# Two kilobytes of one key load, taken as a load of 119 rows and a load of 9 rows

## The chip, the cores and the metric

The kernel runs on one NeuronCore of one Trainium2 chip. The metric is the device time of one execution in microseconds (us), as the median of several runs; lower is better. The core has five engines that run on their own (TensorE, in the profile PE, with its weight loads as PEld; VectorE, DVE; ScalarE, ACT; GpSimd, POOL; SyncE, SP) and 16 DMA engines that move data between HBM and the on-chip memory SBUF, which has 128 partitions.

## What is computed

One decode step (one new token for each of 4 sequences) goes through two layers. Both layers use the same weights and the same caches: layer norm, grouped-query attention over a cache of 4096 positions with 32 query heads and 8 key/value heads, a residual, layer norm, a SwiGLU feed-forward block, a residual.

```
def _A_ref(x, k_cache, v_cache, wq, wo):
    q = (x @ wq).reshape(B, Sq, Hq, Dh).transpose(0, 2, 1, 3)
    k = jnp.repeat(k_cache, rep, axis=1)
    v = jnp.repeat(v_cache, rep, axis=1)
    scores = jnp.einsum("bhqd,bhkd->bhqk", q, k) * (Dh ** -0.5)
    p = _softmax(scores, axis=-1)
    o = jnp.einsum("bhqk,bhkd->bhqd", p, v)
    return o.transpose(0, 2, 1, 3).reshape(B, Sq, Hq * Dh) @ wo

def _B_ref(x, w1, w3, w2):
    h = _silu(x @ w1) * (x @ w3)
    return h @ w2

for layer in range(2):
    x = x + _A_ref(_layernorm(x), A_k_cache, A_v_cache, A_wq, A_wo)
    x = x + _B_ref(_layernorm(x), B_w1, B_w3, B_w2)
```

Everything is float32: B = 4, D = 512, Hq = 32, Hkv = 8, Sk = 4096, Dh = 128, F = 1792.

## The kernel before

All weights and both caches lie in one HBM array of 128 rows (`rows`), in the order in which layer 0 uses them. Positions in it are counted in units (`KB` = 256 float32, so 1 KB of each row, 128 KB over all rows). On the chip one tile, `space`, of 218 such units per partition takes all that is loaded. The table `LOADS` (lines 52 to 66) sets by hand every transfer of the program in order: first unit in HBM, number of units, first unit in `space`. A second pass over the table's later half reads most of the data again for layer 1, which goes through the groups backwards, from group 7 to group 0.

`pump` (lines 120 to 144) walks the table: as long as the next entry's place in `space` is free, it issues that transfer on SP's DMA queue (line 140) and notes where each tile now lies. `done` frees a tile's units after its last use in a layer and calls `pump` again. So the order of the transfers is that of the table, and the moment of each is that at which the engine that last read the place has finished. The table's entry `(320, 64, 28)` is the transfer which the change touches: 64 units, 64 KB of each row, 8192 KB in all, to units 28 to 91 of `space`.

A group's keys are 64 units: 16 tiles of 4 units, 8 for each of two steps. So this entry holds all the keys of group 2, and its last two units (382 and 383) are the second half of the last tile of the second step. `score` (line 311) multiplies a step's key tiles with the queries, two matmuls for each tile, one for each half; `maximum`, `exponent` and `turn` make the softmax weights of it, and `weigh` (line 381) multiplies them with the group's values. Each layer ends with `feed_forward`, whose last part, `down` (line 499), reads the units of `w2` as they land (matmuls on line 503). Then DVE copies the result (line 599) and SP stores it (line 600).

Of the kernel before, what the change touches and what calls it, by code (L numbers as in the profile page):

```python
# [16 lines left out]
P = 128  # L17
# [25 lines left out]
KB = 256  # L43
# [16 lines left out]
    (868, 8, 68), (876, 4, 186), (880, 4, 190), (884, 8, 194), ("stash", 1, 202), (892, 8, 206), ("stash", 0, 214),  # L60
# [5 lines left out]
)  # L66
BUSY = (4, 1, 2)
SCRATCH = 64

# [5 lines left out]
def tile_decode_layers(ctx: ExitStack, tc: tile.TileContext, rows, out):  # L75
    nc = tc.nc
# [9 lines left out]
    def place(at, n):  # L86
        return space[:, at * KB:(at + n) * KB]
# [32 lines left out]
    def pump():  # L120
        while state["next"] < len(LOADS):
            src, n, at = LOADS[state["next"]]
            if src == "stash":
                i, n = n, U // KB
                keys = [("kv", TURN, i)]
                if i == 0 and not state["back"]:
                    return
            else:
                keys = [key for key in stream if src <= offset[key] < src + n]
            if any(taken[at:at + n]):  # L130
                return
            taken[at:at + n] = [True] * n
            if src == "stash":
                for j in range(2):
                    nc.scalar.activation(place(at, n)[:, j * BLOCK:(j + 1) * BLOCK], stored[2 * i + j], AF.Copy)
            elif state["next"] == 0:
                nc.sync.dma_start(space[:, at * KB:], rows[:, 0:n * KB + P])
            else:
                lo = src * KB + (P if src >= LOADS[0][1] else 0)
                nc.sync.dma_start(place(at, n), rows[:, lo:lo + n * KB])  # L140
            for key in keys:
                where[key] = at
                at += size[key[0]]
            state["next"] += 1
# [4 lines left out]
    def done(layer, *key):  # L149
        if layer == 0 and (key[0][:2] == "w1" or key[0] in ("wq", "wo") and key[1] >= HELD or key[:2] == ("kv", TURN) and key[2] in KEPT):  # L150
            return
        at, n = where[key], size[key[0]]
        taken[at:at + n] = [False] * n
        pump()

    pump()


# [40 lines left out]
    def busy(n):  # L199
        if n:  # L200
            pt = scores().rearrange("p (k c) -> p k c", k=KC)
            nc.tensor.matmul(pt[:, 0:n, :], ident, ident.unsqueeze(1).to_broadcast([P, n, P]),  # L202
                             start=True, stop=True)
# [31 lines left out]
    def layernorm():  # L235
        xc, sq = deviation()
        xT = lay_down(xc)
        squares(xc, sq)

        def factor():  # L240
            var = o_ps[1][:, 1:2]
            mean(var, ssq)
            inverse(rstd[:, 0:1], var)

        return xT, factor
# [173 lines left out]
    def turn_o(o, oT):  # L419
        nc.tensor.matmul(misc[:, 0:B * REP], o, head, start=True, stop=True)  # L420
        nc.vector.tensor_copy(oT[:, :, 0:B], misc[:, 0:B * REP].rearrange("p (b h) -> p h b", b=B))  # L421
# [5 lines left out]
    def project_o(layer, g, oT):  # L427
        w = wo_of(g)
        for h in range(REP):
            for k in range(KC):  # L430
                nc.tensor.matmul(x_ps[32 * k:32 * k + B, :], oT[:, h, 0:B], w[:, h, k * P:(k + 1) * P],  # L431
                                 start=(h == 0), stop=(h == REP - 1))
        done(layer, "wo", g)
        nc.vector.scalar_tensor_tensor(x_sb, x_ps, 1.0, x_sb, op0=ALU.mult, op1=ALU.add,
                                       accum_out=rowsum)
# [107 lines left out]
    for layer in range(LAYERS):  # L543
# [13 lines left out]
        for n, (g, (first, last)) in enumerate(order):  # L557
# [7 lines left out]
            if layer and n == 0:  # L565
                state["back"] = True
                pump()
# [22 lines left out]
        nc.scalar.activation(spare, half[:, 0:1], AF.Sigmoid)  # L590
        busy(BUSY[0])
        turn_o(o, oT)
        busy(BUSY[1])
        project_o(layer, g, oT)
        busy(BUSY[2])
        xT, factor = layernorm()
# [50 lines left out]
```

## Time and profile before

| what | value |
|---|---|
| median of 3 runs | 704.12 us (704.09 to 704.31) |
| the profiled execution, its own time | 704.12 us |
| its span, first to last instruction | 702.3 us |
| mean granted clock of TensorE | 0.825 |
| PE, PEld busy | 421.3 us, 133.4 us |
| DVE, ACT, POOL busy | 144.5 us, 41.7 us, 3.1 us |
| read from HBM | 297.34 MB |

The 1.8 us between the span and the execution's own time lie outside the profiled instructions. Times in the views below are microseconds from the start of the span. In a table of windows each row is a stretch of time: the busy time of each engine in it, the granted clock of PE, and the mean busy share of the 16 DMA engines with what they moved in GB/s. In a list of DMA queues a row has the packets, the MB and the time that the packets took as a share of 16 engines.

### The profile page before, as it was taken

Reading aid. Unit: us, or ns where it says so; the run is one execution under the profiler, and the core shown is the slowest. Engines: PE = TensorE matmul, PEld = TensorE weight load, DVE = VectorE, ACT = ScalarE, POOL = GpSimd, SP = SyncE. Lnnn points to the kernel's source line nnn. Section 1 sums busy time; section 2 is a strip of 40 time slices with the busy share of each in tenths; the row PEclk is TensorE's granted clock in tenths of the full one; section 3 lists DMA queues with packets and bytes.
Section 4 is the critical chain, followed back from the end, with each engine's and each line's share of the span. In section 5 each row is a group of like instructions: output and inputs, shape, how many; then the busy total and the mean of one; then the engine's idle time right before and its main releaser. Section 6 shows DMA issues by size and latency. Waiting matters only on the chain.

```text
span 702.3 us, 7502 instructions
## 1 busy us (share of the span) xinstructions
PE 421.3 (60%) x3280; PEld 133.4 (19%) x3280; DVE 144.5 (21%) x512; ACT 41.7 (6%) x100; POOL 3.1 (0%) x10
## 2 busy tenths in 40 slices
PE   1265466644578409667688985744555734567576
PEld 0111121201112103121124221201111211121223
DVE  2012112121023103330231322112120301213221
ACT  0010000100001001000101210000100001000100
POOL 0000000000000000000000000000000000000000
PEclk9997677876769859886999997877877958779999
DMA  9999999999999999999999999999999999999996
GB/s 422 418 415 425 467 419 418 426 457 417 449 414 444 424 438 415 436 423 427 422 418 378 423 430 440 439 438 418 441 440 414 450 419 448 430 425 417 424 425 268
DMA packets 12991, 297.87 MB, mean 424 GB/s; under 512 B 1440, under 2 KB 1568, under 8 KB 4512
## 3 DMA queue, kind: packets, MB, share of 16 engines
q1 hardware_dynamic: 12960, 297.41, 99.0%
q8 instruction: 25, 0.41, 0.2%
q14 instruction: 6, 0.05, 0.0%
HBM read 297.34 MB, written 0.07 MB: 423 GB/s over the span
## 4 chain that ended last, share of the span: by engine, by line
DMA 71%; PE 24%; DVE 1%; another core or an unknown queue 1%; ACT 1%; issue 1%; SPq 0%; ACTq 0%; DVEq 0%
DMA space<-in_rows 71%; PE o L387 10%; PE scores L322 9%; PE sums_ps L306 1%; PE turned L348 1%; ACT p L341 1%; PE scores L202 1%; PE stored L251 1%; DVE acc L335 0%; DVE pT L350 0%; PE o L463 0%; SPq L140 0%; PE sums_ps L431 0%; PE sums_ps L420 0%
## 5 line engine op out<-in xcount | busy, mean ns | idle before, releaser
L322 PE MATMUL scores<-space,qT 128*32 128x512 f32 x1024 | 170.0, 713 | 141.6 <-DMA space<-in_rows 140.8
L387 PE MATMUL o<-space,pT 128*16 128x512 f32 x1024 | 152.8, 710 | 99.3 <-DMA space<-in_rows 91.5
L322 PEld LDWEIGHTS scores<-space,qT 128*32 128x32 f32 x1024 | 36.0, 123 | 218.6 <-issue 180.0
L387 PEld LDWEIGHTS o<-space,pT 128*16 128x16 f32 x1024 | 31.7, 108 | 198.3 <-issue 94.2
L335 DVE TENSOR_REDUCE acc<-scores 128x1 f32<-128x512 f32 x32 | 22.1, 691 | 181.5 <-PE scores L322 181.5
L341 ACT ACTIVATE p<-scores,acc 128x512 f32<-128x512 f32 x30 | 20.6, 687 | 559.0 <-DVE acc L335 432.1
L410 DVE SCALAR_TENSOR_TENSOR o<-o,acc,o 128x128 f32<-128x128 f32 x112 | 39.3, 351 | 49.2 <-PE o L387 45.8
L350 DVE COPY pT<-turned 128x256 f32<-128x256 f32 x32 | 13.6, 425 | 154.3 <-PE turned L348 154.3
L348 PE MATMUL turned<-ident,p 128*128 128x128 f32 x128 | 21.9, 296 | 11.8 <-ACT p L341 11.8
L295 PE MATMUL sums_ps<-space,xT 128*32 128x512 f32 x120 | 22.9, 704 | 2.4 <-DMA space<-in_rows 2.4
L421 DVE COPY o<-sums_ps 128x16 f32<-128x16 f32 x16 | 2.8, 175 | 98.1 <-PE sums_ps L420 98.1
L348 PEld LDWEIGHTS turned<-ident,p 128*128 128x128 f32 x128 | 14.0, 145 | 44.1 <-ACT p L341 25.7
L306 PEld LDWEIGHTS sums_ps<-same,shares 128*128 128x128 f32 x120 | 16.3, 211 | 16.8 <-DVE shares L301 11.1
L306 PE MATMUL sums_ps<-same,shares 128*128 128x4 f32 x120 | 17.6, 270 | 0.9 <-DVE shares L301 0.9
L463 PE MATMUL o<-space,xT 128*32 128x192 f32 (+1 forms) x256 | 13.7, 355 | 3.2 <-DMA space<-in_rows 1.5
L441 PE MATMUL stored<-space,o 128*32 128x512 f32 x104 | 13.5, 592 | 0.0
L301 DVE TENSOR_SCALAR shares<-sums_ps,columns 128x512 f32<-128x512 f32 x15 | 11.1, 743 | 1.7 <-PE sums_ps L295 1.7
L503 PE MATMUL sums_ps<-space,hT 128*4 128x128 f32 x224 | 9.1, 272 | 3.6 <-DMA space<-in_rows 2.9
L211 PE MATMUL o<-columns,same 128*32 128x1 f32 x64 | 2.0, 181 | 14.3 <-DVE columns L548 13.3
L420 PEld LDWEIGHTS sums_ps<-columns,o 128*128 128x128 f32 x32 | 6.1, 239 | 20.6 <-issue 13.0
L463 PEld LDWEIGHTS o<-space,xT 128*32 128x32 f32 x256 | 7.6, 110 | 8.4 <-DVE h L480 2.8
L420 PE MATMUL sums_ps<-columns,o 128*128 128x16 f32 x32 | 7.7, 318 | 0.6 <-DVE o L410 0.6
(101 smaller groups left out, 141.9 us busy)
## 6 DMA issues: line engine op xcount, KB each, us to landing
space<-in_rows SPq DMA_DIRECT2D x11, 4096.0 KB, 21.6
space<-in_rows SPq DMA_DIRECT2D x14, 1024.0 KB, 18.6
space<-in_rows SPq DMA_DIRECT2D x3, 4608.0 KB, 24.6
space<-in_rows SPq DMA_DIRECT2D x2, 6144.0 KB, 30.9
space<-in_rows SPq DMA_DIRECT2D x6, 2048.0 KB, 29.2
space<-in_rows SPq DMA_DIRECT2D x3, 3584.0 KB, 23.5
space<-in_rows SPq DMA_DIRECT2D x2, 5120.0 KB, 28.7
space<-in_rows SPq DMA_DIRECT2D x1, 7680.0 KB, 33.8
```

Source lines behind the costliest of these rows:

```text
L295: nc.tensor.matmul(wide[32 * k:32 * k + 32, :], xT[:, 32 * k:32 * k + 32], w[:, k, :], start=True, stop=True)
L306: nc.tensor.matmul(misc[:, h * B:(h + 1) * B], shares[:, h * DH:(h + 1) * DH], same[:, 0:B], start=True, stop=True)
L322: nc.tensor.matmul(ps[32 * b:32 * b + 32, :], qT[:, b, at:at + 32], t[:, i * BLOCK:(i + 1) * BLOCK], start=(m < 2), stop=(m >= TILES - 2))
L335: nc.vector.tensor_reduce(acc[:, i:i + 1], ps, axis=AX.X, op=ALU.max, negate=True)
L341: nc.scalar.activation(p.rearrange("p n s -> p (n s)"), ps, AF.Exp, bias=acc[:, i:i + 1], scale=1.0 if scale is None else scale, accum_out ...
L348: nc.tensor.transpose(pt[:, n, :], p[:, n, :], ident)
L350: nc.vector.tensor_copy(pT, pt.rearrange("p n (b r) -> p n b r", b=B)[:, :, :, 0:ROW])
L387: nc.tensor.matmul(o_ps[i][32 * b:32 * b + ROW, :], pT[:, r // 2, b, :], t[:, j * NB * DH:(j + 1) * NB * DH], start=(r < 2), stop=(r >= TI ...
L410: nc.vector.scalar_tensor_tensor(o, o_ps[s][:, j * DH:(j + 1) * DH], acc[:, 16 + NB * s + j:17 + NB * s + j], o, op0=ALU.mult, op1=ALU.add)
L420: nc.tensor.matmul(misc[:, 0:B * REP], o, head, start=True, stop=True)
L441: nc.tensor.matmul(bank[32 * h:32 * h + 32, :], oT[:, h, :], w[:, h, :], start=first, stop=last)
L463: nc.tensor.matmul(bank[32 * j:32 * j + 32, s], xT[:, 32 * k:32 * k + 32], w[:, j], start=(k == 0), stop=(k == KC - 1))
```

## The change

The entry of 64 units becomes one of 62 units and one of 2 units, next to each other both in HBM and in `space`. A new table, `APART`, says for an entry how many of the 128 rows its first transfer takes; the remaining rows go in a second one. It has the one entry 382: 119.

```
@@ LOADS
-    (580, 28, 190), (320, 64, 28), (8, 24, 92), ...
+    (580, 28, 190), (320, 62, 28), (382, 2, 90), (8, 24, 92), ...
+APART = {382: 119}
@@ pump
                 lo = src * KB + (P if src >= LOADS[0][1] else 0)
-                nc.sync.dma_start(place(at, n), rows[:, lo:lo + n * KB])
+                cut = APART.get(src, P)
+                for rs in (slice(0, cut), slice(cut, P)):
+                    if rs.start < P:
+                        nc.sync.dma_start(place(at, n)[rs], rows[rs, lo:lo + n * KB])
```

All other entries have no row in `APART` and are issued as before, in one transfer of 128 rows. The same bytes go to the same places.

On SP's queue the entry stands among the loads of layer 1's groups 2 and 1. Each row is one transfer: rows of SBUF by float32 elements, and in brackets the semaphores that SP waits for ahead of it (`DMAHW` those of earlier transfers, `PE` those of matmuls). Before:

```order
L140 DMA space<-in_rows 128x9216 [waits DMAHW3_49,DMAHW1_49,PE_49]
L140 DMA space<-in_rows 128x7168 [waits PE_49]
L140 DMA space<-in_rows 128x16384 [waits DMAHW2_49,PE_49]
L140 DMA space<-in_rows 128x6144 [waits PE_49]
L140 DMA space<-in_rows 128x16384 [waits DMAHW4_49,DMAHW3_49,PE_49]
L140 DMA space<-in_rows 128x16384 [waits DMAHW5_49,DMAHW0_49,PE_49]
```

And with the change, where the transfer's line is 144:

```order
L144 DMA space<-in_rows 128x9216 [waits DMAHW3_49,DMAHW1_49,PE_49]
L144 DMA space<-in_rows 128x7168 [waits PE_49]
L144 DMA space<-in_rows 128x15872 [waits DMAHW2_49,PE_49]
L144 DMA space<-in_rows 119x512 [waits PE_49]
L144 DMA space<-in_rows 9x512
L144 DMA space<-in_rows 128x6144 [waits DMAHW0_49,PE_49]
L144 DMA space<-in_rows 128x16384 [waits DMAHW4_49,DMAHW3_49,PE_49]
```

The one transfer of 16384 elements has become three that follow each other, and every later one has moved back by two places; transfers take the eight `DMAHW` semaphores in turn, so the names behind it are shifted by two.

On PE the place is the end of group 2's second step in layer 1 and the start of its values. Before:

```order
L306 MATMUL sums_ps<-same,shares 128x4 [waits DVE_49]
L306 MATMUL sums_ps<-same,shares 128x4 x3
L322 MATMUL scores<-space,qT 32x512 x10
L387 MATMUL o_94<-space,pT 16x512 [waits DMAHW7_49]
L387 MATMUL o_94<-space,pT 16x512 x15
```

And with the change, with four lines more ahead of each:

```order
L310 MATMUL sums_ps<-same,shares 128x4 [waits DVE_49]
L310 MATMUL sums_ps<-same,shares 128x4 x3
L326 MATMUL scores<-space,qT 32x512 x9
L326 MATMUL scores<-space,qT 32x512 [waits DMAHW7_49,DMAHW6_49]
L391 MATMUL o_94<-space,pT 16x512 [waits DMAHW1_49]
L391 MATMUL o_94<-space,pT 16x512 x15
```

The step's last matmul, the only one that reads units 382 and 383, now waits for the two small transfers. The order of the matmuls is the same.

2 rows, old and new, of the table LOADS are left out of this document.

## The prediction

> **What bounds the kernel now.** I read the busy slices and the DMA queues first, then the chain of waits, then windows over the second half and over the last ten microseconds.
>
> ```profile
> DMA packets 12991, 297.87 MB, mean 424 GB/s; under 512 B 1440, under 2 KB 1568, under 8 KB 4512
> q1 hardware_dynamic: 12960, 297.41, 99.0%
> q8 instruction: 25, 0.41, 0.2%
> DMA 71%; PE 24%; DVE 1%; another core or an unknown queue 1%; ACT 1%; issue 1%; SPq 0%; ACTq 0%; DVEq 0%
> ```
>
> The loads' packets take 99.0% of the time of all 16 DMA engines, and the chain that ended last is 71% DMA. PE is busy for 60% of the span and mostly waits for loads. In the part that the change can touch, from 500 us on, the engines have no gaps:
>
> ```profile
> 500.00:560.00 60.00, 34.81 (x253) 9.90 (x252) 13.83 (x52) 2.93 (x8) 0.00 (x0) 0.80 1.00 432
> 560.00:600.00 40.00, 14.08 (x98) 4.40 (x102) 3.43 (x10) 1.85 (x5) 0.00 (x0) 0.67 1.01 436
> 600.00:640.00 40.00, 25.84 (x170) 7.25 (x174) 7.89 (x28) 1.85 (x5) 0.00 (x0) 0.80 0.98 424
> 640.00:690.00 50.00, 37.94 (x372) 13.56 (x364) 14.66 (x55) 3.97 (x8) 0.55 (x1) 0.91 1.00 424
> ```
>
> The next to last number is the DMA share: 0.98 to 1.01. So from here on the time is set by how long each DMA engine needs for the packets still dealt to it, and not by when a load is issued. The end of the chain says the same:
>
> ```profile
> 686.24 12.80 DMA space<-in_rows
> 699.03 0.04 issue
> 699.08 0.45 PE sums_ps L503 x8
> 699.55 0.29 DVE space L599
> ```
>
> The last load (512 elements of each row, 256 KB) is issued at 686.24 us and has landed at 699.03; alone it would take 0.26 MB / 424 GB/s = 0.6 us, so it stood behind some 12 us of older packets. What follows its landing, to the span's end, is 702.3 - 699.03 = 3.3 us and does not depend on the change.
>
> Now the windows over that landing:
>
> ```profile
> 690.00:693.00 3.00, 2.11 (x41) 1.16 (x39) 0.74 (x3) 0.00 (x0) 0.00 (x0) 1.00 1.00 410
> 694.50:695.00 0.50, 0.13 (x8) 0.00 (x0) 0.04 (x1) 0.00 (x0) 0.00 (x0) 1.00 0.75 295
> 695.00:695.50 0.50, 0.23 (x10) 0.22 (x14) 0.00 (x0) 0.00 (x0) 0.00 (x0) 1.00 0.65 242
> 695.50:696.00 0.50, 0.50 (x28) 0.49 (x20) 0.00 (x0) 0.00 (x0) 0.00 (x0) 1.00 0.60 225
> 696.00:696.50 0.50, 0.33 (x13) 0.04 (x4) 0.00 (x0) 0.00 (x0) 0.00 (x0) 1.00 0.51 197
> 696.50:697.00 0.50, 0.39 (x16) 0.36 (x16) 0.00 (x0) 0.00 (x0) 0.00 (x0) 1.00 0.44 172
> 697.00:697.50 0.50, 0.23 (x11) 0.00 (x0) 0.00 (x0) 0.00 (x0) 0.00 (x0) 1.00 0.26 98
> 697.50:698.00 0.50, 0.22 (x9) 0.22 (x13) 0.00 (x0) 0.00 (x0) 0.00 (x0) 1.00 0.20 74
> 698.00:698.40 0.40, 0.40 (x16) 0.11 (x4) 0.00 (x0) 0.00 (x0) 0.00 (x0) 1.00 0.12 46
> 698.40:698.80 0.40, 0.28 (x8) 0.14 (x8) 0.00 (x0) 0.00 (x0) 0.00 (x0) 1.00 0.03 10
> ```
>
> Times 16, the shares are engines still at work: 16 at 692, 12.0 at 694.75, 8.2 at 696.25, 4.2 at 697.25, 1.9 at 698.2, 0.5 at 698.6. The engines do not finish together. From 694.5 to 699.03 they idle for 0.5 x (0.25 + 0.35 + 0.40 + 0.49 + 0.56 + 0.74 + 0.80) + 0.4 x (0.88 + 0.97) + 0.23 = 2.8 us on average while the last one or two finish. **The last engine sets the end, and the mean engine is done 2.8 us sooner.** That is also the most which any other dealing of these bytes could gain.
>
> **Why some are late.** The loads are dealt evenly: 12960 packets in 90 transfers are 144 each, 128 rows and 16 packets under 512 B (1440 / 90), one for each engine. What is not even is the instruction queue: 25 pieces of 16 KB over the run, three of them after 652 us:
>
> ```profile
> q8 instruction: 3, 0.05, 0.4%
> ```
>
> In that window of 47 us they take 0.4% x 16 x 47 = 3.0 us, 1.0 us for each. Spread over all 16 engines 25 pieces would be one or two each, and the engines would end about 1 us apart. They end over 4 us apart (694.5 to 699.0), so I take it that the pieces fall on some of the engines, about half, three or so on each. Which engines those are, no view tells.
>
> **The change part by part.** (1) The long load shrinks from 64 to 62 KB a row. Each engine has 8 of its rows, so each loses 8 x 2048 B = 16.4 KB; at 432 / 16 = 27.0 GB/s that is 0.61 us off every engine.
>
> (2) The 119 rows of 2 KB. No transfer before has other than 128 rows, so their dealing is bounded. Equal shares, as every load shows, exist for 119 = 7 x 17 only on 7 engines (17 rows each) or on one. The lower bound is a deal over all 16 as if it were even: nothing for the two parts together. The upper one is a single engine. I take 7 x 17, the nearest to what the rows show.
>
> A row's price comes from the stretch in which short loads run:
>
> ```profile
> 379.00:381.00 2.00, 1.82 (x36) 1.14 (x36) 0.00 (x0) 0.00 (x0) 0.00 (x0) 1.00 1.02 366
> ```
>
> At 366 / 16 = 22.9 GB/s for each engine, 2048 B take 0.09 us; at the long rows' 27.0 they take 0.076. So 17 rows cost 1.29 to 1.52 us.
>
> (3) The 9 rows, in equal shares: one on each of 9 engines, 0.08 to 0.09 us.
>
> [...]
>
> Sum for each kind of engine: the seven get -0.61 + 1.29 to 1.52, and 0.08 to 0.09 where they also hold one of the 9 rows: **+0.76 to +1.0 us, taken as +0.85**. An engine with only one of the 9 rows gets **-0.52**, one with neither **-0.61 us**. What the nine lose, the seven carry.
>
> (4) SP issues two transfers more. The stretch in question:
>
> ```profile
> 545.36 64.68 SPq L140 DMA_DIRECT2D space<-in_rows  x5
> 573.39 3.64 PE L322 MATMUL scores<-space,qT 128*32 128x512 f32 x16 [15.40 <-DMA space<-in_rows]
> 585.28 2.77 PE L322 MATMUL scores<-space,qT 128*32 128x512 f32 x20
> 599.95 5.87 PE L387 MATMUL o<-space,pT 128*16 128x512 f32 x32 [11.91 <-DMA space<-in_rows]
> L140 SPq DMA_DIRECT2D space<-in_rows x88: 327/328/1182, 1.2 to 686.2; - x88
> ```
>
> An issue takes 0.33 us (median) and SP issues five loads in 65 us here; the engines hold older packets meanwhile (share 1.00). Nothing, then; if that cover were gone it would be 0.66 us. What stands behind them on SP is the load of 6144 elements, which has its own wait for PE.
>
> (5) PE's new wait. The load's keys are first used at 573.39, when it has landed. The small rows stand right behind it, so they land by 573.4 + 1.5 = 575 us. The matmul that now waits for them is the last of the run that starts at 585.28 and ends at 588.05. Some 12 us cover it, and PE idles for 11.91 us right after, until 599.95. So the wait costs nothing, even if an engine carried all the rows.
>
> So the sum hangs on one question: is the engine that ends last one of the nine or one of the seven? With 1.9 engines left at 698.2, the last two lie within a microsecond of each other. Drawn at random both are among the nine with 9/16 x 8/15 = 0.30; if the burdened engines are one block of neighbours, as the split itself makes two blocks, nearly 9/16 = 0.56. Since the pieces seem to fall on half of the engines only, I go nearer to the block. Then the last ones end 0.52 to 0.61 us sooner, and the seven, of which the last would be among those done by 696.5, still end before them (696.5 + 1.0 = 697.5 against 698.5).
>
> [...] The windows here show late engines, but no numbers of them.
>
> **Forecast: 704.12 - 0.55 = 703.6 us**, from the profiled execution, whose time is the median of the runs.
>
> **Rivals.** *A late engine is among the seven (slower).* The place is the same landing at 699.03: the last engine then gets +0.85 us, 705.0 us (704.7 to 705.9, where the seven also hold each other up as their 17 rows go to other partitions than usual). It decides as soon as any of the seven is within 0.85 us of the last. For it: 1.9 engines are left at 698.2, 3.2 at 697.75. Against: the seven are the smaller part.
>
> [...]
>
> *One engine takes all 119 rows.* 119 x 0.09 - 0.61 = 10.1 us; it may have been up to 4.5 us ahead (694.5 against 699.03), so the end moves by 5.6 to 10.1 us: 709.7 to 714.2 us. Against: every load of the trace is dealt to 16.
>
> *The relief also moves a late instruction piece past the end of an engine's loads.* That adds its 1.0 us and the wait around it to the 0.6: 702.4 us. For it: the queue's last pieces fall within the last 47 us. Against: PE asks for them by its own progress, which hardly moves.
>
> **How the numbers follow.** Forecast 0.47, a late engine among the seven 0.32, nothing moves 0.09, one engine 0.06, a piece moved 0.06. A measurement of this kernel tells about 0.2% (1.4 us) from no change: that is below 702.7 or above 705.5. Faster by more: the last rival, 0.06. Slower by more: the one engine, 0.06, and the top of the second case, 0.09. Within: 0.79. The forecast's own range is 703.4 to 703.9. For 8 in 10 the range takes in the second case up to 705.4 and goes down to 703.3.
>
> **What would show it.** Right: the list of queues has 128 packets of 2 KB more, PE's idle time ahead of the values of group 2 stays near 12 us, and the windows over the last landing show the same staircase with its foot 0.5 to 0.6 us earlier and its first steps later. The second case: the foot is about 0.85 us later. One engine: a share of 0.06 for several microseconds at the end. The forecast's reasoning is wrong if the share falls below 0.97 anywhere between 560 and 690 us, or if the tail behind the last landing is not 3.3 us.

## The result

| | before | with the change |
|---|---|---|
| median of 21 runs | 704.22 us | 705.91 us (705.10 to 707.13) |
| ratio, with 95% interval | | 1.0022 (1.0016 to 1.0028) |
| the profiled execution, its own time | 704.12 us | 705.10 us |
| its span | 702.3 us | 703.3 us |

The change makes the kernel slower, by 1.1 to 2.0 us. The forecast was 703.6 us, and the measured median lies outside the range of 703.3 to 705.4. The profiled execution is at the short end of the changed kernel's runs: of the 1.7 us between the medians it holds 1.0.

The list of DMA queues of the changed kernel has the packets:

```profile
DMA packets 13135, 297.87 MB, mean 424 GB/s; under 512 B 1456, under 2 KB 1584, under 8 KB 4656
q1 hardware_dynamic: 13104, 297.41, 99.1%
```

The loads' queue has 144 packets more than the 12960 of before: 128 rows of 2 KB, and 16 small ones (1456 against 1440). An ordinary load has 16 small packets (1440 / 90), taken here as one for each of its engines; the two new transfers together have 16. With equal shares on each engine only 7 + 9 gives that. So the rows went to 7 engines and to 9, as the prediction dealt them.

Now the windows over the place of the change (stretch in us, its length, PE, PEld, DVE, ACT, POOL busy, granted clock, DMA share, GB/s). Before:

```profile
560.00:569.00 9.00, 0.00 (x0) 0.00 (x0) 0.00 (x0) 0.00 (x0) 0.00 (x0) 0.51 1.03 445
569.00:576.00 7.00, 2.60 (x16) 0.69 (x16) 0.00 (x0) 0.00 (x0) 0.00 (x0) 0.50 0.89 380
576.00:600.00 24.00, 11.47 (x90) 3.71 (x86) 3.43 (x10) 1.85 (x5) 0.00 (x0) 0.78 1.04 450
```

With the change:

```profile
560.00:569.00 9.00, 0.00 (x0) 0.00 (x0) 0.00 (x0) 0.00 (x0) 0.00 (x0) 0.63 1.05 445
569.00:576.00 7.00, 2.17 (x12) 0.68 (x16) 0.00 (x0) 0.00 (x0) 0.00 (x0) 0.50 0.88 275
576.00:600.00 24.00, 12.59 (x86) 3.85 (x78) 3.42 (x10) 1.85 (x5) 0.00 (x0) 0.78 1.04 447
600.00:640.00 40.00, 24.63 (x162) 6.96 (x162) 7.88 (x28) 1.85 (x5) 0.00 (x0) 0.79 0.98 425
```

Read the second row of each. The engines are as busy as before (0.88 against 0.89), yet they move 275 GB/s in place of 380. The time is not lost by waiting for a load to be issued: the packets themselves take longer, those of the ordinary loads around them too. The trace has the time of every packet: between 569 and 576 us a 24 KB packet of the load that follows takes 1.24 us (median), before it was 0.91. From 569 to 600 us before moved 380 x 7 + 450 x 24 = 13.46 MB, the change 275 x 7 + 447 x 24 = 12.65 MB. The 0.81 MB that are missing take 0.81 / 424 GB/s = 1.9 us of all 16 engines later on. From 600 us on the rates are equal again (425 and, before, 424 GB/s between 600 and 640 us).

The end of the chain, and the windows over it:

```profile
686.97 12.91 DMA space<-in_rows
699.88 0.04 issue
699.92 0.45 PE sums_ps L507 x8
700.39 0.29 DVE space L603
```

```profile
694.50:695.00 0.50, 0.50 (x15) 0.30 (x17) 0.15 (x2) 0.00 (x0) 0.00 (x0) 1.00 0.90 361
695.00:695.50 0.50, 0.36 (x16) 0.07 (x4) 0.26 (x3) 0.00 (x0) 0.00 (x0) 1.00 0.98 389
695.50:696.00 0.50, 0.00 (x0) 0.00 (x0) 0.00 (x0) 0.00 (x0) 0.00 (x0) 1.00 0.98 389
696.00:696.50 0.50, 0.48 (x20) 0.47 (x24) 0.00 (x0) 0.00 (x0) 0.00 (x0) 1.00 0.85 340
696.50:697.00 0.50, 0.50 (x24) 0.28 (x12) 0.00 (x0) 0.00 (x0) 0.00 (x0) 1.00 0.79 307
697.00:697.50 0.50, 0.21 (x12) 0.16 (x12) 0.00 (x0) 0.00 (x0) 0.00 (x0) 1.00 0.76 274
697.50:698.00 0.50, 0.49 (x16) 0.19 (x8) 0.00 (x0) 0.00 (x0) 0.00 (x0) 1.00 0.55 209
698.00:698.40 0.40, 0.00 (x0) 0.00 (x0) 0.00 (x0) 0.00 (x0) 0.00 (x0) 1.00 0.49 169
698.40:698.80 0.40, 0.29 (x12) 0.29 (x16) 0.00 (x0) 0.00 (x0) 0.00 (x0) 1.00 0.23 77
698.80:699.20 0.40, 0.33 (x13) 0.04 (x4) 0.00 (x0) 0.00 (x0) 0.00 (x0) 1.00 0.21 77
699.20:699.60 0.40, 0.23 (x8) 0.14 (x8) 0.00 (x0) 0.00 (x0) 0.00 (x0) 1.00 0.03 10
```

The last load lands at 699.88 us, 0.85 later than before; the tail behind it is 3.4 us, before it was 3.3. The staircase has its first steps much later: 12.2 engines are at work around 697.25 us where there were 4.2. Idle time up to the last landing is 0.5 x (0.10 + 0.02 + 0.02 + 0.15 + 0.21 + 0.24 + 0.45) + 0.4 x (0.51 + 0.77 + 0.79 + 0.97) + 0.28 = 2.1 us for the mean engine, against 2.8. So the mean engine finishes at 697.8 us in place of 696.3: **1.5 us later, while the last one is 0.85 us later.** Rows that only moved from nine engines to seven would have left the mean where it was.

### The profile page after: what moved, and what is told of

It reads as the page before. It is cut to its first block, busy times and chain, and to the rows that moved or that the text cites. A ratio compares the mean times of both kernels' runs of the same rounds, so it can differ in the third digit from the quotient of the medians.

```text
span 703.3 us, 7507 instructions
## 1 busy us (share of the span) xinstructions
PE 417.1 (59%) x3280; PEld 133.5 (19%) x3280; DVE 144.5 (21%) x512; ACT 41.7 (6%) x100; POOL 3.0 (0%) x10
## 2 busy tenths in 40 slices
DMA packets 13135, 297.87 MB, mean 424 GB/s; under 512 B 1456, under 2 KB 1584, under 8 KB 4656
## 4 chain that ended last, share of the span: by engine, by line
DMA 71%; PE 24%; DVE 2%; another core or an unknown queue 1%; ACT 1%; issue 1%; SPq 0%; ACTq 0%; DVEq 0%
DMA space<-in_rows 71%; PE scores L326 11%; PE o L391 8%; PE sums_ps L310 2%; PE turned L352 1%; ACT p L345 1%; PE sums_ps L299 1%; PE stored L255 1%; DVE acc L339 0%; DVE o L414 0%; PE o L467 0%; PE sums_ps L435 0%; SPq L144 0%; PE scores L206 0%
## 5 line engine op out<-in xcount | busy, mean ns | idle before, releaser
L326 PE MATMUL scores<-space,qT 128*32 128x512 f32 x1024 | 168.3, 707 | 146.5 <-DMA space<-in_rows 145.8
L391 PE MATMUL o<-space,pT 128*16 128x512 f32 x1024 | 148.4, 691 | 97.3 <-DMA space<-in_rows 90.5
```

The source lines that it names most:

```text
L326: nc.tensor.matmul(ps[32 * b:32 * b + 32, :], qT[:, b, at:at + 32], t[:, i * BLOCK:(i + 1) * BLOCK], start=(m < 2), stop=(m >= TILES - 2))
L391: nc.tensor.matmul(o_ps[i][32 * b:32 * b + ROW, :], pT[:, r // 2, b, :], t[:, j * NB * DH:(j + 1) * NB * DH], start=(r < 2), stop=(r >= TI ...
```

## The experiments

Theory A: rows that are dealt in other shares than those of a 128-row load go to partitions that other engines are writing to, and so slow engines that have nothing to do with the change. The expectations call the places in SBUF where engines would then meet receivers; they are an assumption of the author, and no view shows one. Theory B is the prediction's second case: only the seven are late. Theory C: rows of 2 KB behind long ones are slow by themselves. The edits below are parts of each kernel's difference to the changed kernel, or to another kernel that the text names.

**Two units on their own, all 128 rows.**

```
-APART = {382: 119}
+APART = {}
```

> The two units are a load of their own, but of all 128 rows in one transfer. Theory A (rows that are dealt in other shares than the 128-row deal write to partitions that other DMA engines are writing to, and so slow all 16): as before, 704.1 to 704.6 us, and in the 7 us around the landing of group 2's keys the DMA engines move about 380 GB/s as before. Theory B (only the seven engines with 17 rows are late): 704.1 to 704.4 us. Theory C (short rows behind long ones are slow by themselves): 705.5 to 706 us, as the change.

Measured: 704.29 us, ratio to before 1.0001 (0.9992 to 1.0010). The same stretch in its windows:

```profile
569.00:576.00 7.00, 3.27 (x16) 0.69 (x16) 0.00 (x0) 0.00 (x0) 0.00 (x0) 0.50 0.93 394
576.00:600.00 24.00, 11.15 (x86) 3.82 (x86) 3.43 (x10) 1.85 (x5) 0.00 (x0) 0.78 1.04 448
```

No dip: 394 GB/s where before moved 380. A load more, rows of 2 KB and the wait on PE cost nothing that can be measured, and a 2 KB row takes 0.084 us (median), within the prediction's 0.076 to 0.09; in the changed kernel it takes 0.127. Theory C falls; what costs is the division of the rows.

**112 and 16 rows: equal shares.**

```
-APART = {382: 119}
+APART = {382: 112}
```

> The two units as 112 rows and 16 rows: in equal shares 7 rows and 1 row on each of 16 engines, so no engine has more than another, but the rows fall on other engines than in a load of 128. Theory A: slower than before by some 0.5 to 1.5 us (704.7 to 705.7), with the dip in GB/s around 570 to 575 us. Theory B: 704.1 to 704.4 us, no dip. Theory C: 705.5 us and more.

Measured: 705.80 us, ratio 1.0028 (1.0019 to 1.0037).

```profile
569.00:576.00 7.00, 2.17 (x12) 0.68 (x16) 0.00 (x0) 0.00 (x0) 0.00 (x0) 0.50 0.97 324
576.00:600.00 24.00, 12.74 (x86) 3.85 (x78) 3.42 (x10) 1.85 (x5) 0.00 (x0) 0.78 1.02 438
```

The trace has 1472 small packets, 32 more than before, so each of the two transfers went to 16 engines. With equal shares each engine carries the same bytes as before, and the loss, a little above the 705.7 us of the expectation, is as large as with the change. Theory B falls as the explanation; uneven shares are not needed. That the rows fall on other engines than in a load of 128 is the author's assumption; no view shows the engine of a row. The missing bytes are 13.46 - (324 x 7 + 438 x 24 = 12.78) = 0.68 MB, 1.6 us.

**119 and 9 rows of four units.**

```
-    (320, 62, 28), (382, 2, 90),
+    (320, 60, 28), (380, 4, 88),
-APART = {382: 119}
+APART = {380: 119}
```

> Four units instead of two are taken as 119 and 9 rows. Theory A: the loss doubles, 1.6 to about 3.2 us over before: 707 to 707.8 us, with a dip of twice the length. Theory B: the seven engines get 1.5 to 2.0 us instead of 0.76 to 1.0: 705.6 to 706.2 us. Theory C: as the change plus a little, 706 to 706.5 us.

Measured: 707.93 us, ratio 1.0051 (1.0037 to 1.0064).

```profile
569.00:576.00 7.00, 2.19 (x12) 0.69 (x16) 0.00 (x0) 0.00 (x0) 0.00 (x0) 0.50 0.93 215
576.00:600.00 24.00, 13.92 (x86) 4.09 (x78) 3.42 (x10) 1.85 (x5) 0.00 (x0) 0.78 1.02 434
```

Missing: 13.46 - 11.92 = 1.54 MB, 3.6 us, where the end is 3.9 us later. The loss grows with the bytes that are dealt this way, slightly more than the expectation had it. Over the four kernels the end goes with the bytes missing in these 31 us: about 0, 1.6, 1.9 and 3.6 us by the windows, 0.3, 1.8, 1.7 and 3.9 us between medians (128, 112 + 16, 119 + 9, and 119 + 9 of four units). The traced executions, from which the windows are, are 0.0, 1.4, 1.0 and 4.0 us longer than the traced one of before, so the missing bytes are a rough measure: for the change they are too high by 0.9.

**The whole load as 64 and 64 rows.** The entry of 64 units is whole again, and goes in two halves.

```
-    (320, 62, 28), (382, 2, 90),
+    (320, 64, 28),
-APART = {382: 119}
+APART = {320: 64}
```

> The whole load of 64 units goes as 64 rows and 64 rows, 4 rows on each of 16 engines twice, with long rows of 64 KB. Theory A, if the receivers of 64 neighbouring rows are half of all: each half runs at half speed, the load takes up to 19 us more, and the end is 10 to 19 us later: 714 to 723 us. Theory B: equal shares, 704.1 to 704.5 us. Theory C: long rows, 704.1 to 704.5 us.

Measured: 727.04 us, ratio 1.0322 (1.0303 to 1.0341). One window from the middle of the load:

```profile
570.00:580.00 10.00, 0.00 (x0) 0.00 (x0) 0.00 (x0) 0.00 (x0) 0.00 (x0) 0.50 1.00 210
```

The mean busy share of the 16 engines is 1.00 and they move 210 GB/s, half of the mean of 424. A 64 KB packet takes some 5.1 us here (median), in an ordinary load 2.42. The loss, 23.0 us, was more than expected.

**The same, read from one piece of HBM.** The edit is against the run with 64 and 64 rows. For each half 64 rows are read from the start of the array in one piece; the keys of group 2 in layer 1 are then other values.

```
-    nc.sync.dma_start(place(at, n)[rs], rows[rs, lo:lo + n * KB])
+    source = rows[rs, lo:lo + n * KB]
+    if src in APART:
+        flat = rows.rearrange("p w -> (p w)")
+        source = flat[0:cut * n * KB].rearrange("(p f) -> p f", p=cut)
+    nc.sync.dma_start(place(at, n)[rs], source)
```

> As the run with 64 and 64 rows of the whole load, but what is read for each half is one contiguous piece of HBM from the array's start, so group 2's keys of layer 1 are other values than the cache's. The receiving side (SBUF partitions) sets the loss: again about 727 us (725 to 729). The reading side (where the rows lie in HBM) sets it: back to 704 to 710 us.

Measured: 727.31 us, and again:

```profile
570.00:580.00 10.00, 0.00 (x0) 0.00 (x0) 0.00 (x0) 0.00 (x0) 0.00 (x0) 0.50 1.00 210
```

Where these rows lie in HBM makes no difference (727.31 against 727.04 us, 210 GB/s in both). That points to the side of SBUF, for which the run with 16 rows to HBM below speaks too.

**Four times 32 rows, and eight times 16 rows.** The load of 64 units goes in pieces of `cut` rows, with 32 or 16 in the table (the edit of `pump`, against the run with 64 and 64 rows):

```
-    for rs in (slice(0, cut), slice(cut, P)):
-        if rs.start < P:
-            nc.sync.dma_start(place(at, n)[rs], rows[rs, lo:lo + n * KB])
+    for r0 in range(0, P, cut):
+        nc.sync.dma_start(place(at, n)[r0:r0 + cut], rows[r0:r0 + cut, lo:lo + n * KB])
```

> The whole load as four transfers of 32 neighbouring rows, 2 rows on each of 16 engines. [...] Theory A with receivers of neighbouring rows (32 rows reach a quarter): some 58 us more than before, 760 us. Cost for each transfer of its own: 705 us.

> The whole load as eight transfers of 16 neighbouring rows, one row on each engine. [...] Cost for each transfer of its own, no receivers: 705 to 707 us.

Measured: 727.63 us with 32 rows, 756.13 us with 16. The window of the first, then one of the second:

```profile
570.00:580.00 10.00, 0.00 (x0) 0.00 (x0) 0.00 (x0) 0.00 (x0) 0.00 (x0) 0.50 1.00 210
```

```profile
580.00:590.00 10.00, 0.00 (x0) 0.00 (x0) 0.00 (x0) 0.00 (x0) 0.00 (x0) 0.50 1.03 131
```

32 neighbouring rows are as fast as 64 (210 GB/s in both, half of the mean of 424); the four transfers in place of two cost 0.6 us between the medians. A quarter of the rate with 32 rows, by which the end would have been at 760 us, did not occur. 16 rows reach 131 GB/s in this window (111 to 151 in those of 10 us from 570 to 610), and over the whole load, if all of the loss is its own, 8.39 MB / (19.8 + 52.1 us) = 117 GB/s, 0.28 of 424. So against the mean of 424 GB/s, with transfers of 128 rows, the load went at 210 in transfers of 64 and of 32 rows and at some 117 in transfers of 16; no view shows what sets these steps.

**The whole load as 112 and 16 rows.** Against the run with 64 and 64 rows:

```
-APART = {320: 64}
+APART = {320: 112}
```

> [...] Theory A: between nothing and the 23 us of 64 and 64 rows, more likely the upper part: 710 to 725 us, since each engine writes through several receivers in turn and meets others there. Theory B (uneven shares alone): 704.1 to 704.6 us.

Measured: 728.10 us, above the 710 to 725 us that theory A was given. The reason that theory A gives, engines that meet at receivers, no view shows. The rates:

```profile
565.00:570.00 5.00, 0.00 (x0) 0.00 (x0) 0.00 (x0) 0.00 (x0) 0.00 (x0) 0.50 1.04 303
570.00:580.00 10.00, 0.00 (x0) 0.00 (x0) 0.00 (x0) 0.00 (x0) 0.00 (x0) 0.50 1.06 236
580.00:590.00 10.00, 0.00 (x0) 0.00 (x0) 0.00 (x0) 0.00 (x0) 0.00 (x0) 0.50 1.07 134
```

236 and 303 GB/s while the 112 rows run, 134 at their end and in the 16. So a load that is neither small nor, if 112 and 16 rows are dealt here as in the run of two units, uneven is slowed as well. What slows it was not shown.

**Extra bytes that do not go to SBUF.** Is the prediction's premise right, that the engines that end last are among the nine? The kernel before gets one transfer more behind group 2's keys, from HBM to a scratch place in HBM: 7 rows of 32 KB, then 16 rows, then 7 rows of 64 KB.

```
+    aside = nc.dram_tensor("aside", (7, 32 * KB), F32, kind="Internal").ap()
     nc.sync.dma_start(place(at, n), rows[:, lo:lo + n * KB])
+    if (src, n) == (320, 64):
+        nc.sync.dma_start(aside, rows[0:7, 0:32 * KB])
```

> The kernel before with one transfer more right behind group 2's keys: 7 rows of 32 KB go from HBM to a scratch place in HBM, one row on each of 7 engines, and meet no partition of SBUF. Each of the seven gets 32.8 KB / 27.0 GB/s = 1.2 us more, if writing is no slower than reading. If the engines that end last are among the other nine, as the prediction took it: 704.0 to 704.4 us. If they are among the seven: 704.9 to 705.4 us.

> The same with 16 rows of 32 KB, one on each of 16 engines, as the measure of the price: each engine, the last one too, gets 1.2 us more: 705.2 to 705.5 us in any case.

> The kernel before with 7 rows of 64 KB set aside to HBM: 2.4 us more on each of the seven engines, none on the others. The prediction read from the windows that the seven are done by about 696.5, 2.5 us ahead of the last: 704.0 to 704.5 us. If the seven have less room than that, the end moves by the difference: up to 706 us.

Measured: 704.09 us with 7 rows, ratio 1.0000 (0.9991 to 1.0009); 705.33 us with 16 rows, 1.0017 (1.0008 to 1.0025); 705.86 us with 7 rows of 64 KB, 1.0029 (1.0019 to 1.0039). The packets of the first:

```profile
DMA packets 13005, 298.10 MB, mean 424 GB/s; under 512 B 1447, under 2 KB 1575, under 8 KB 4519
```

14 more than before: 7 rows and 7 small ones, so 7 engines, taken here to be the seven that get the 119 rows; no view numbers the engines. They take 1.2 us more, by the estimate of the expectation, and the end does not move; with the same bytes on each of all 16 it moves by 1.3 us. So the engines that end last are among the other nine. The double amount moves it: the last landing of the trace is at 700.05 us, 1.0 later than before. The seven have room for 1.2 us but not for 2.4 (some 1.4 by this trace), less than the 2.5 which the prediction read from the staircase and the expectation's first case took over. The median moves by 1.7 us, more than that room explains; this part stays open.

The run with 16 rows also bears on theory A: each of its 32 KB packets takes 1.22 us, as the 32 KB packets of ordinary loads do, though a transfer has only one row for each engine. 16 rows into SBUF took 8.17 us for each 64 KB packet, against 2.42. So in these runs few rows in a transfer are slow on their way into SBUF, and not on their way to HBM.

**The change once more.**

> The changed kernel once more, for a second trace, since its first profiled execution (705.1 us) was the shortest of its runs. Theory A: some 275 GB/s between 569 and 576 us again, and the end at 705.1 to 706.9 us. If the dip is deeper here and the end later by as much, the spread of its runs comes from the dip; if the dip is the same and the end later, it comes from behind it.

Measured: 705.16 us, in the same stretch:

```profile
569.00:576.00 7.00, 2.45 (x12) 0.68 (x16) 0.00 (x0) 0.00 (x0) 0.00 (x0) 0.50 0.91 279
```

The dip repeats, and so does the time of the first trace. Both traces are of executions at the short end; what makes others of the 21 runs up to 2 us longer is in neither, and stays open.

## Why the prediction was wrong

*What bounds the kernel.* Right: from 500 us on the loads alone set the time (the DMA share is 0.98 and 1.00 between 600 and 690 us, before and with the change), bytes that are not moved in one stretch come back as time at the end, and the tail hardly changed (3.3 and 3.4 us). But the sign that the prediction named, a busy share below 0.97, does not tell the kernels apart: from 569 to 576 us the share is 0.88 with the change and 0.89 before. The rate does.

*How the rows are dealt (2, 3).* Right: 7 and 9 engines, by the count of small packets (1456 against 1440), if the shares are equal. Which engines they are no view shows.

*Which engines are late.* Right, by the run with 7 rows set aside, if its seven engines are those of the 119 rows. The reasoning from the instruction pieces was not tried by itself, so that part may be luck.

*SP's issues and PE's wait (4, 5).* Right: the plain load of two units has both kinds of change and costs nothing. In the changed kernel PE idles 12.18 us ahead of group 2's values, before it was 11.91.

*The price of the rows.* This is the step that failed: "the seven get -0.61 + 1.29 to 1.52" and "one with neither **-0.61 us**". It priced the 128 rows by the stretch with short loads of 128 rows, and put the price on the engines that carry them alone. That price holds where the 128 rows go in one transfer (0.084 us a row). Divided, a row takes 0.127 us, and the 24 KB packets of the ordinary load beside it 1.24 us in place of 0.91, a cost for which the sum has no term. It makes the mean engine 1.5 us later by the staircase, 1.9 by the windows, and the relief of 0.5 to 0.6 us for the nine stands against it. The runs fit theory A as far as it says that divided rows slow other loads too and that the loss lies on the way into SBUF. Where the engines meet there was not shown.

*The sum as it should have been.* An estimate, if the loss falls on all engines alike, which no view shows: for the nine 1.5 to 1.9 less 0.55, +0.95 to +1.35 us. For the seven 1.5 to 1.9 and 0.85, less their room of at least 1.2: at most +1.15 to +1.55. The end came 1.0 us later in the traced executions and 1.7 by the medians. Which engine is last in the changed kernel was not shown.

*The rivals.* The 0.09 for "nothing moves" has no run behind it: the runs show the end 1.7 us later by the medians, and the loads beside the divided rows slowed. The case of a late engine among the seven gave 704.7 to 705.9 us, and the measured median lies at the top edge. That top stood for the seven holding each other up because their rows go to other partitions than usual, which no view shows; it slowed the seven alone, while 112 + 16 rows, without any seven, cost as much. The single engine with 119 rows did not occur, and between 652 and 699 us there are three instruction pieces, as before.

## What to carry to other kernels

On a DMA stream without gaps, ask of each transfer not only how many bytes each engine gets but how many of the 128 rows it takes: of the deals tried here only that of all 128 rows kept the 424 GB/s, and a division of the rows, even or not, held up the other loads too. Rows that are taken off a late engine can cost it more than they relieve it: with 119 and 9 rows the relief was an estimated 0.6 us and the price 1.5 to 1.9 us for the mean engine. A kernel's bytes per microsecond in a window at an equal busy share show such a loss at once, long before the end of the chain does.

## What was not expected of the hardware

The busy share says nothing of the speed: 1.00 stood beside 424, 210 and (1.03) 131 GB/s. Half of the rows in one transfer halved the rate even with 64 KB rows and a busy share of 1.00, and the loss is larger than the load itself (23.0 us for a load that takes 8.39 MB / 424 GB/s = 19.8). And 112 + 16 rows, of which the 112 are seven eighths of all, were no better than 64 + 64: 728.1 against 727.0 us.
